# Decode attention with an MLP beside it on one core: the last 4 KB of each row of w1 in three loads of 112, 8 and 8 rows

## The chip, the core and the metric

The kernel runs on one core of one Trainium2 chip. The metric is the time of one execution in device microseconds; for the kernel before it is the median of three runs. The core has five engines that run beside each other: TensorE (PE; PEld is its weight load), VectorE (DVE), ScalarE (ACT), GpSimd (POOL) and SyncE (SP), which here does nothing but issue loads. Sixteen DMA engines move the data between HBM and the on-chip buffers, which have 128 rows (partitions).

## The reference

One token `x` of 512 values is normalised, and two branches are added to it: attention over a cache of 65536 positions, with 32 query heads on 8 heads of keys and values, and an MLP with 1792 hidden values and a ReLU.

```python
x  = A_x                                   # 1 x 512
xn = layernorm(x)
q  = (xn @ wq) as 32 heads of 128          # wq: 512 x 4096
o  = softmax(q k^T * 128**-0.5) v          # k, v: 8 x 65536 x 128; 4 query heads share one of them
y  = x + o @ wo + relu(xn @ w1) @ w2       # wo: 4096 x 512, w1: 512 x 1792, w2: 1792 x 512
```

All is float32. The cache has 2 x 268 MB, the four weights 24 MB together, and there is one token: nearly every byte is read once and used once.

## The kernel before

The program is one function; the engines' programs stand in it one after another, and semaphores by name tie them together. SP issues all the large loads into three buffers, in the order in which the data is used (lines 151 to 179): the three pieces of wq into `kt`, all of w1 into `wt` with one load (line 160), then k and v by turns, 32 pieces of each, k into `kt` and v into `vt`, then wo into `kt`, and w2 in five pieces into `wt`. Each piece of k or v has 128 rows of 64 KB, 8.39 MB. A load counts its semaphore up by 16 when it has landed.

What sets the order around the change is SP's own order: its loads go into one queue, and each DMA engine takes its share of them in that order. SP waits only where a buffer is to be free: `kfree` (line 161, for the first piece of k, when PE is through with wq; then in each turn, when the scores of a piece of k are worked out), `vfree` (line 164), and `hT` (line 174) before w2 overwrites `wt`. At the end it waits for `y` and stores the result.

The row of w1 that lies in a partition has four parts of 1792 values, one for each of the four values of `xn` in that partition. POOL waits for the semaphore `w1` (line 217), multiplies each part by its value of `xn` (line 219) and adds the four to one row of 1792 values (lines 222 to 224), which ends with semaphore `sum`. PE sums that row over the partitions with matmuls by ones (line 281), three times over in each turn, as `PASSES` says, while DVE and ACT do the softmax; the first of them waits for `sum`.

In each turn PE does the matmuls of the scores (line 313), DVE transposes them (366) and takes the maximum (384), ACT takes the exponentials (256), and PE multiplies them with v (292). At the end PE adds the rows of w2 (lines 331 and 339, which wait for each of its five pieces), DVE transposes the sum (417), and SP stores it.

Of the kernel before, what the change touches and what calls it, by code (L numbers as in the profile page):

```python
# [15 lines left out]
DFF_ALL = 1792  # L16
# [21 lines left out]
XA = D // P  # L38
# [6 lines left out]
W2_SUM = 12  # L45
W2_ROWS = 10
PASSES = 3


def take(e, sem, n=1):  # L50

    return e.sem_inc(sem, -n).wait_op(sem, n, "sem-ge")  # L52
# [7 lines left out]
def attention_and_mlp_kernel(  # L60
# [12 lines left out]
    sp, pe, dve, act, pool = nc.sync, nc.tensor, nc.vector, nc.scalar, nc.gpsimd  # L73
    scale = float(DH) ** -0.5

    def sbuf(name, *shape):
        return nc.alloc_sbuf_tensor(name, list(shape), F32).ap()
# [3 lines left out]
    def sem(name):  # L81
        if name not in sems:
            sems[name] = nc.alloc_semaphore(name)
        return sems[name]
# [7 lines left out]
    wt = sbuf("wt", P, FB * D)  # L92
# [47 lines left out]
    w1_row = w1.rearrange("p a f -> p (a f)")  # L140
# [16 lines left out]
    for i in range(1, len(WQ_CUTS)):  # L157
        cut = slice(wq_at[i], wq_at[i + 1])
        sp.dma_start(kt[:, cut], wq_row[:, cut]).then_inc(sem(WQ_SEMS[i]), 16)  # L159
    sp.dma_start(wt, w1_row).then_inc(sem("w1"), 16)  # L160
    take(sp, sem("kfree"))
    sp.dma_start(kt, k[0, 0]).then_inc(sem("k"), 16)
    with sp.Fori(0, NCH - 1) as n:
# [50 lines left out]
    after(pool.tensor_copy(qpad[:, :XA], xn), "pool", chain[0]).then_inc(sem("q"), 1)  # L214
    f = DFF_ALL
    w1_of = [wt[:, a * f : (a + 1) * f] for a in range(XA)]
    pool.wait_ge(sem("w1"), 16)
    for a in range(XA):
        last = pool.tensor_scalar_mul(w1_of[a], w1_of[a], xn[:, a : a + 1])  # L219
    last.then_inc(sem("pool"), 1)  # L220
# [50 lines left out]
    with nc.body("turns", valid_engines=[pe.engine]):  # L271
# [3 lines left out]
        with pe.If(t > 1):  # L275
            after(pe.transpose(pma[:GROUP, :P], m, ident), "d2p").then_inc(sem("p2d"), 1)  # L276
            after(pe.matmul(pmb[:, :GROUP], ones[:GROUP, :], dg, start=True, stop=True), "d2p", 2).then_inc(sem("p2d"), 1)  # L277

            with pe.Fori(0, PASSES):
                for c in range(CT):  # L280
# [175 lines left out]
```

## Time and profile before

| what | value |
|---|---|
| time, median of three runs | 1303.06 us (1302.93 to 1303.19) |
| the profiled execution, first to last instruction (span) | 1301.3 us |
| read from HBM | 560.99 MB, 431 GB/s over the span |
| busy, share of the span: PE | 60% |
| busy: DVE, ACT, POOL | 21%, 6%, 3% |
| DMA engines, in the queue that SP feeds | 99.7% |

The profile has no time of its own for the profiled execution beside its span; the span leaves out what lies ahead of the first instruction and behind the last, and is 1.8 us under the median of the runs. Times in the views are microseconds from the start of the span. A load is shown where it is issued, with the time until it landed; a wait on a load is shown at the instruction that waited.

### The profile page before, as it was taken

To read this page: it belongs to the slowest core of one execution; us is meant where nothing else is said; L and a number is where in the kernel's file an instruction comes from. 1 tells how busy PE (TensorE), PEld (TensorE's weight loads), DVE (VectorE), ACT (ScalarE), POOL (GpSimd) and SP (SyncE) were. 2 spreads that over 40 slices of the span, in tenths; PEclk is the share of its full clock that TensorE was granted. 3 is DMA by queue.
4 is the path that set the end of the run, shared out by engine and by line. 5 is a ranking of instruction groups with operands and counts; after the bars stand their busy time and mean duration, and the time that the engine had idled before them with its cause. 6 is when DMAs were issued, how large, how long until landed. Compare 5 with 4: busy or idle time off the path is not lost.

```text
span 1301.3 us, 13055 instructions
## 1 busy us (share of the span) xinstructions
PE 774.9 (60%) x5474; PEld 231.1 (18%) x5474; DVE 274.8 (21%) x466; ACT 76.2 (6%) x299; POOL 34.8 (3%) x30
## 2 busy tenths in 40 slices
PE   3365674665576456566555566666567466557557
PEld 1111121111121111121111121111112111112112
DVE  2211222211222220222220122221122221122222
ACT  1000000000000000000000000000000000000000
POOL 1900000000000000000000000000000000000000
PEclk9677877776887777786776777677777777777779
DMA  9999999999999999999999999999999999999998
GB/s 403 451 419 451 419 451 419 435 435 419 451 419 451 419 451 419 449 421 423 447 419 451 419 451 419 451 419 435 435 419 451 419 451 419 451 419 443 427 420 370
DMA packets 11236, 561.02 MB, mean 431 GB/s; under 512 B 1505, under 2 KB 1505, under 8 KB 1890
## 3 DMA queue, kind: packets, MB, share of 16 engines
q1 hardware_dynamic: 11088, 561.00, 99.7%
q10 hardware_dynamic: 146, 0.00, 0.0%
q8 instruction: 1, 0.02, 0.0%
q14 instruction: 1, 0.01, 0.0%
HBM read 560.99 MB, written 0.00 MB: 431 GB/s over the span
## 4 chain that ended last, share of the span: by engine, by line
issue 94%; DMA 3%; POOL 2%; SPq 0%; PE 0%; DVE 0%; POOLq 0%
DMA wt<-w 3%; POOL wt L219 1%; POOL wt L224 0%; POOL wt L222 0%; POOL wt L223 0%; SPq L177 0%; SPq L159 0%; PE banks L339 0%; DVE ysb L417 0%; SPq L151 0%; POOL hT L226 0%; SPq L452 0%; POOLq L156 0%
## 5 line engine op out<-in xcount | busy, mean ns | idle before, releaser
L313 PE MATMUL banks<-kt,qpad 128*32 128x512 f32 x2176 | 310.0, 733 | 311.1 <-PEq L52 308.7
L292 PE MATMUL banks<-vt,probs 128*16 128x512 f32 x2048 | 271.3, 690 | 82.1 <-PEq L52 82.1
L366 DVE STREAM_TRANSPOSE tr<-banks 128x1024 f32<-128x1024 f32 x136 | 170.0, 1250 | 471.4 <-PE banks L313 466.8
L313 PEld LDWEIGHTS banks<-kt,qpad 128*32 128x32 f32 x2176 | 84.5, 131 | 509.6 <-issue 496.3
L281 PE MATMUL banks<-wt,ones 128*1 128x448 f32 x768 | 121.3, 786 | 0.0
L292 PEld LDWEIGHTS banks<-vt,probs 128*16 128x16 f32 x2048 | 68.4, 108 | 298.4 <-issue 298.4
L392 DVE COPY o_sb<-banks 128x512 f32<-128x512 f32 x32 | 22.1, 692 | 455.3 <-PE banks L292 455.3
L254 ACT ACTIVATE corr<-diff 128x8 f32<-128x8 f32 x32 | 6.7, 208 | 1179.8 <-ACTq L52 1179.8
L256 ACT ACTIVATE probs<-tr,nb_new 128x128 f32<-128x128 f32 x128 | 65.3, 521 | 0.0
L276 PE MATMUL banks<-ident,m 128*4 128x128 f32 x32 | 9.7, 303 | 78.9 <-DVE m L384 78.9
L302 PE MATMUL banks<-sel,o_sb 128*128 128x4 f32 x256 | 32.8, 252 | 18.7 <-PEq L52 18.7
L302 PEld LDWEIGHTS banks<-sel,o_sb 128*128 128x128 f32 x256 | 31.0, 191 | 20.6 <-issue 20.6
L226 POOL TENSOR_SCALAR hT<-ysum 128x14 f32<-128x14 f32 x1 | 0.3, 257 | 1220.7 <-DVE ysum L404 1220.7
L384 DVE TENSOR_REDUCE m<-tr 128x4 f32<-128x512 f32 x32 | 32.2, 1006 | 2.9
L281 PEld LDWEIGHTS banks<-wt,ones 128*1 128x1 f32 x768 | 20.2, 100 | 58.9 <-issue 58.4
L277 PE MATMUL banks<-dg,ones 4*128 4x4 f32 x64 | 15.4, 309 | 20.0 <-DVE dg L387 20.0
L256 ACT ACTIVATION_READ_ACCUMULATOR probs<-tr,nb_new 128x1 f32 x128 | 24.0, 187 | 0.0
L276 PEld LDWEIGHTS banks<-ident,m 128*4 128x4 f32 x32 | 2.6, 81 | 108.0 <-DVE m L384 108.0
L219 POOL TENSOR_SCALAR wt<-wt,xn 128x1792 f32<-128x1792 f32 x4 | 19.1, 4797 | 16.5 <-DMA wt<-w 16.5
L277 PEld LDWEIGHTS banks<-dg,ones 4*128 4x128 f32 x64 | 12.6, 245 | 27.1 <-DVE dg L387 27.1
L299 PEld LDWEIGHTS banks<-part_sum,ones 128*128 128x128 f32 x64 | 9.5, 188 | 27.2 <-issue 27.2
L395 DVE TENSOR_TENSOR lo_run<-lo_run,banks 128x8 f32<-128x8 f32 x32 | 5.2, 163 | 40.0 <-DVEq L52 40.0
(69 smaller groups left out, 91.1 us busy)
## 6 DMA issues: line engine op xcount, KB each, us to landing
kt<-wq SPq DMA_DIRECT2D x2, 2048.0 KB, 9.3
kt<-wq SPq DMA_DIRECT2D x1, 4096.0 KB, 20.8
kt<-wo SPq DMA_DIRECT2D x1, 4096.0 KB, 15.5
kt<-wo SPq DMA_DIRECT2D x2, 2048.0 KB, 22.2
wt<-w SPq DMA_DIRECT2D x1, 3584.0 KB, 28.9
wt<-w SPq DMA_DIRECT2D x1, 1536.0 KB, 9.5
wt<-w SPq DMA_DIRECT2D x1, 1024.0 KB, 11.7
kt<-k SPq DMA_DIRECT2D x32, 24.1
```

The lines of the kernel that those rows point to most:

```text
L219: last = pool.tensor_scalar_mul(w1_of[a], w1_of[a], xn[:, a : a + 1])
L256: last = act.activation(probs[:, :, g], tr[:, :, g], AF.Exp, bias=nb_new[:, g : g + 1], scale=scale, accum_out=part_sum[:, g : g + 1],)
L276: after(pe.transpose(pma[:GROUP, :P], m, ident), "d2p").then_inc(sem("p2d"), 1)
L277: after(pe.matmul(pmb[:, :GROUP], ones[:GROUP, :], dg, start=True, stop=True), "d2p", 2).then_inc(sem("p2d"), 1)
L281: ins = pe.matmul(hrow[32 * c : 32 * c + 1, :], ones[:, :1], hb[:, :, 32 * c : 32 * c + 32], start=True, stop=True,)
L292: last = pe.matmul(acc[c : c + WIDE * GROUP, :], probs[:, b : b + WIDE, :].rearrange("p b g -> p (b g)"), vt[:, b * DH : (b + WIDE) * DH], ...
L299: pe.matmul(lo_new[:, 0, :], ones, part_sum, start=True, stop=True).then_inc(sem("vfree"), 1)
L302: last = pe.matmul(lo_new[:, 1, :], o_sb[:, b, :], sel[:, b, :], start=(b == 0), stop=(b == WIDE - 1),)
L313: last = pe.matmul(pair[s // 2 % 2][32 * c : 32 * c + 32, s % 2 * 512 : s % 2 * 512 + 512], qpad, kb[:, s * 16 : s * 16 + 16, c, :], start ...
L366: ins = after(dve.transpose(tr2[:, s * 1024 : (s + 1) * 1024], pair[s % 2]), "p2d", s + 1)
L384: dve.reduce_max(m, tr.rearrange("p b i -> p i b")[:, :GROUP, :], axis=AX.X).then_inc(sem("d2p"), 1)
L392: after(dve.tensor_copy(o_sb.rearrange("p b d -> p (b d)"), acc), "p2d", 7).then_inc(sem("d2p"), 1)
```

## The change

The load of w1 is cut in two at 24 KB of each row's 28 KB. The first 24 KB of all 128 rows come as one load. The last 4 KB of each row (1024 values) come as three loads: of rows 0 to 111, of rows 112 to 119, and of rows 120 to 127. All four count the same semaphore, and POOL waits for 64 in place of 16. Bytes, destinations and all else stay as they were. By the words of the change, eight DMA engines are to have nine rows of the 4 KB pieces and eight seven, where a load of 128 rows gives each engine eight.

```diff
+W1_REST = 1024
+W1_ROWS = [slice(0, 112), slice(112, 120), slice(120, 128)]
...
-    sp.dma_start(wt, w1_row).then_inc(sem("w1"), 16)
+    wide = XA * DFF_ALL - W1_REST
+    sp.dma_start(wt[:, :wide], w1_row[:, :wide]).then_inc(sem("w1"), 16)
+    for rows in W1_ROWS:
+        sp.dma_start(wt[rows, wide:], w1_row[rows, wide:]).then_inc(sem("w1"), 16)
     take(sp, sem("kfree"))
     sp.dma_start(kt, k[0, 0]).then_inc(sem("k"), 16)
...
-    pool.wait_ge(sem("w1"), 16)
+    pool.wait_ge(sem("w1"), 16 + 16 * len(W1_ROWS))
```

On SP, between the last load of wq and the first load of v, the kernel before has these instructions (the shape is that of the part of the buffer that is written; the ISA row is a change of a semaphore):

```order
L159 DMA kt<-wq 128x4096
L159 DMA kt<-wq 128x8192
L160 DMA wt<-w 128x7168
L162 DMA kt<-k 128x16384
L163 UNCONDITIONAL_BRANCH
L165 ISA
L165 DMA vt<-v 128x16384
```

And in the same place the changed kernel, whose lines stand two to five further down:

```order
L161 DMA kt<-wq 128x4096
L161 DMA kt<-wq 128x8192
L163 DMA wt<-w 128x6144
L165 DMA wt<-w 112x1024
L165 DMA wt<-w 8x1024 x2
L167 DMA kt<-k 128x16384
L168 UNCONDITIONAL_BRANCH
L170 ISA
L170 DMA vt<-v 128x16384
```

One instruction has become four; the load of k behind them waits for `kfree` in both. No instruction of another engine has moved.

## Rows read from the trace of the kernel before

**Rows 1.** The page: span, DMA share in forty slices (tenths), SP's queue.

```profile
span 1301.3 us, 13055 instructions
...
DMA  9999999999999999999999999999999999999998
...
q1 hardware_dynamic: 11088, 561.00, 99.7%
```

**Rows 2.** The windows view of the middle, columns named in its first line.

```profile
core 0: us, PE busy (x) PEld busy (x) DVE busy (x) ACT busy (x) POOL busy (x), PEclk, DMA share, GB/s
100.00:1260.00 1160.00, 705.28 (x4950) 210.03 (x4950) 240.60 (x418) 67.13 (x270) 0.00 (x0) 0.75 1.00 434
```

**Rows 3.** The timeline of SP: start, duration, what is issued.

```profile
2.22 0.69 SPq L160 DMA_DIRECT2D wt<-w  x1
26.46 0.33 SPq L162 DMA_DIRECT2D kt<-k  x1
27.18 0.34 SPq L165 DMA_DIRECT2D vt<-v  x1
65.47 0.34 SPq L167 DMA_DIRECT2D kt<-k  x1
77.53 0.33 SPq L165 DMA_DIRECT2D vt<-v  x1
```

**Rows 4.** The lines that load v (first) and k (second), issue to landing.

```profile
L165 SPq DMA_DIRECT2D vt<-v x31: 332/333/343, 27.2 to 1201.6; - x31
...
DMA to landing us min/median/max: 28.4/29.3/42.6
...
L167 SPq DMA_DIRECT2D kt<-k x31: 332/333/343, 65.5 to 1225.9; - x31
...
DMA to landing us min/median/max: 23.5/24.1/25.3
```

**Rows 5.** The chain that ended last, its end: start, duration, what.

```profile
1285.18 12.80 DMA wt<-w
...
1298.02 0.44 PE banks L339 x8
...
1298.49 0.41 DVE ysb L417
```

**Rows 6.** The windows view of the end of the stream, columns as in rows 2.

```profile
1297.00:1297.10 0.10, 0.10 (x14) 0.04 (x4) 0.10 (x1) 0.00 (x0) 0.00 (x0) 1.00 0.96 348
...
1297.20:1297.30 0.10, 0.10 (x8) 0.00 (x0) 0.08 (x1) 0.00 (x0) 0.00 (x0) 1.00 0.26 82
1297.30:1297.40 0.10, 0.10 (x8) 0.07 (x8) 0.00 (x0) 0.00 (x0) 0.00 (x0) 1.00 0.22 82
1297.40:1297.50 0.10, 0.10 (x8) 0.09 (x12) 0.00 (x0) 0.00 (x0) 0.00 (x0) 1.00 0.06 21
```

**Rows 7.** The timeline at the end: PE's weight loads that waited for w2.

```profile
1292.94 0.11 PEld L331 LDWEIGHTS banks<-wt,hT 128*1 128x1 f32 x8 [2.54 <-DMA wt<-w]
...
1295.44 0.16 PEld L331 LDWEIGHTS banks<-wt,hT 128*1 128x1 f32 x8 [0.70 <-DMA wt<-w]
...
1296.72 0.32 PEld L339 LDWEIGHTS banks<-wt,hT 128*1 128x1 f32 x16 [1.12 <-DMA wt<-w]
...
1298.02 0.10 PEld L339 LDWEIGHTS banks<-wt,hT 128*1 128x1 f32 x8 [0.36 <-DMA wt<-w]
```

**Rows 8.** The timeline of ACT's queue: the load of x into one row.

```profile
1.40 0.53 ACTq L235 DMA_DIRECT2D xrow<-x  x1
```

**Rows 9.** The timeline of POOL on w1, and of PE behind it.

```profile
31.17 19.12 POOL L219 TENSOR_SCALAR wt<-wt,xn 128x1792 f32<-128x1792 f32 x4 [16.46 <-DMA wt<-w]
...
58.39 3.99 POOL L224 TENSOR_TENSOR wt<-wt 128x1792 f32<-128x1792 f32 x1
...
64.23 4.66 PE L281 MATMUL banks<-wt,ones 128*1 128x448 f32 x24
69.91 7.06 PE L292 MATMUL banks<-vt,probs 128*16 128x512 f32 x64 [1.02 <-PEq L52]
```

## The prediction

> **What bounds the kernel now.** I read the page first for what is busy: the sixteen DMA engines are at 9 tenths or more in all but the last of the forty slices, and the one queue that SP feeds fills 99.7% of their time [rows 1]. The windows view of the long middle says the same with a rate: DMA share 1.00 at 434 GB/s over 1160 us, which is 27.1 GB/s for one engine, while PE is busy for 705 of the 1160 us [rows 2]. So the time is that of a stream of 561 MB, and it can be lost in two ways only: an engine has nothing queued, or an engine has more to move than the others.
>
> The first does not happen. The issues on SP and the times to landing show it [rows 3, 4]: the first load of v is issued at 27.18 us and lands 42.6 us later (the longest of its kind), at 69.8; the next load of k is issued at 65.47. So 4.3 us before the queue would be empty the next 8 MB is behind it. A load of v is issued 28.4 to 42.6 us before it lands and a load of k 23.5 to 25.3 us, where one of them takes 8.39 MB / 434 GB/s = 19.3 us; the shortest of these covers is 23.5 - 19.3 = 4.2 us.
>
> The second is what the change is about. What ends the program is the last piece of w2: the chain shows it landing 12.80 us after its issue at 1285.18, so at 1297.98, then PE from 1298.02, DVE from 1298.49 and the store [rows 5]. Everything behind that landing is fixed. Since each engine works through its queue without a pause, whatever an engine is given more near the start arrives as a later landing at the end, unless another engine is later anyway. The end of the stream shows how even they are [rows 6]: at 1297.0 to 1297.1 rows of 2 KB still start at 348 GB/s, at 1297.2 to 1297.3 at 82 GB/s (8.2 KB, four rows), at 1297.3 to 1297.4 again four, at 1297.4 to 1297.5 one. An engine starts a row about every 81 ns (below), so after 1297.2 three or four engines are left, and the last of them is 0.2 to 0.3 us behind the bulk. That is all that a perfect evening-out of the engines could give: under 0.3 us of 1303, 0.02%.
>
> **The change, part by part.** Prices first, from loads of 128 rows, so eight rows an engine. PE's weight loads at L331 and L339 wait for the pieces of w2 one after another [rows 7]: the second piece (8 KB rows) is there 2.50 us after the first (1295.44 - 1292.94), so 312 ns a row; the third (4 KB rows) 1.28 us later, so 160 ns a row; the last two (2 KB rows, sixteen rows an engine) 1.30 us later, 81 ns a row. From 4 KB to 8 KB it is 152 ns for 4 KB more, so a row costs 8 ns beside its bytes (160 - 152), or, if this belongs to the load and not to the row, a load costs 8 x 8 = 64 ns.
>
> Moved bytes: an engine had eight rows of 28 KB. Now it has eight of 24 KB, and of the 4 KB rows seven (from the load of 112) or nine (seven, and one from each load of eight rows). Eight engines gain a row, +152 ns; eight lose one, -152 ns.
>
> Added pieces: the seven-row engines have fifteen rows where they had eight and two loads for one: 7 x 8 = 56 ns, or 64 ns. The nine-row engines have seventeen rows and four loads: 9 x 8 = 72 ns, or 3 x 64 = 192 ns. So the seven-row engines come to -0.09 us, and the nine-row engines to +0.22 to +0.34; I take +0.25, nearer to the price by rows, since the rows of 2 KB, with a load for each eight, leave only 81 - 76 = 5 ns.
>
> What this does to the end hangs on which engines are the three or four late ones; no row says. If they are among those with seven rows, they end 0.09 us earlier and the bulk of the others, 0.2 to 0.3 us ahead of them, moves up by 0.25: end between -0.09 and +0.14. If one of them has nine rows, the end is +0.22 to +0.34. I take +0.15 us over both. Below nothing it cannot go by more than the 0.15 us of one row.
>
> Issue on SP: three more instructions. The load of w1 took 0.69 us to issue, the one-row load of x on ACT 0.53 [rows 3, 8]; 3 x 0.69 = 2.1 us at most. SP is then done at about 5.0 us in place of 2.9; its next instruction is held by a semaphore until 26.46, and the engines come to w1 only after wq, whose queue is full until then. Cost nothing; it would cost if wq had landed before 5 us.
>
> The wait on POOL: it waits for all four loads (64 in place of 16), behind it stand four multiplications and three additions, 31.17 to 62.38, and who waits for them is PE at L281, which starts at 64.23 because DVE is that late [rows 9]. So 1.85 us of delay are hidden there, and a further 0.9 us or so between the end of L281 (68.89) and the first matmul on v (69.91). A landing 0.3 us later costs nothing; above 2.7 us the first issue of v would move, which has its own cover (it is issued at 77.53, while the load of k ahead of it lands no sooner than 65.47 + 23.5 = 89.0).
>
> The span is 1301.3 us and the median of the runs is 1303.06, 1.8 us more for what lies around it; the sum goes onto the median: 1303.06 + 0.15 = 1303.2.
>
> **The rivals.** (1) The small loads run slower than their rows in a full load. All loads that this trace prices have 128 rows, and there 27.1 GB/s may be the limit of the engine or of the place where its rows land; the rows cannot tell these apart, because each engine always serves the same sixteenth of the rows. If it is the place, eight neighbouring rows crowd together. Bounds: spread over eight places, 160 ns a load (the forecast); in one place, eight rows in turn, 1.28 us a load, 2 x (1.28 - 0.16) = +2.24 us for both. With two places it is 4 x 160 = 640 ns a load and 2 x 0.48 = +0.96. The engines with nine rows then end 0.96 + 0.25 later than they did, and they are the last; less what they were ahead, +1.0 to +1.2, so 1304.2. For it speaks that engine rate and place rate could not be told apart in any row; against it, that a row shows no such slowing. [...]
>
> (2) Slower by what can be measured: the crowding is complete. Each load of eight rows goes in turn (+2.24), the load of 112 rows, which no longer falls on the engines as 128 rows do, meets itself in pairs (7 x 160 ns = +1.12), and +0.25 as above: +3.6 us, 1306.7. It decides from 2.6 us on. Against it: the sixteen engines never showed such a loss in any slice.
>
> (3) The change does not do what it says: a load of eight rows is given to one engine, not to eight. That engine has 23 rows of 4 KB in place of eight: 15 x 160 = +2.4 us and the pieces, 1305.5. [...]
>
> (4) A gain that can be measured, 2.6 us. The stream has no idle time to give back and the late engines are under 0.3 us behind; I see no mechanism.
>
> **How the numbers follow.** About 0.2% (2.6 us) is what a measurement of this kernel can tell from no change. Forecast 0.55 (1302.95 to 1303.4); rival (1) 0.36 (up to 1304.7 with some of the load of 112 rows slowed too); (3) 0.03; (2) 0.03; another slowing, such as a queue that runs dry, 0.02; (4) 0.01. Forecast and rival (1) together hold 0.91 and lie within 0.2%; with the 0.02 of them that reach further I take 1302.85 to 1304.6 as the range. Rival (3) lies just under the bound and counts as the same, the other slowing half to each side: same 0.91 + 0.03 + 0.01 = 0.95, slower 0.04, faster 0.01.
>
> **What would show it.** In the profile after: the weight loads at L331 and L339 waiting for w2 at the same distances (2.50, 1.28, 1.30 us), all shifted by one amount; the multiplications on POOL starting at about 31.4 if the forecast holds, at 32.2 to 32.5 with two places; the tail of the stream after 1297.2 with about eight engines in it, not four. The forecast is wrong if POOL's start moves by over 0.5 us, and its argument is wrong if POOL's start moves and the end does not, for then the stream has slack that I don't see.

## The result, and the profile after

| | before | changed |
|---|---|---|
| time, median of 21 runs | 1303.31 us | 1305.31 us (1304.87 to 1305.84) |
| ratio, 95% interval | | 1.0016 (1.001 to 1.0021) |
| span of the profiled execution | 1301.3 us | 1303.2 us |

The kernel became 2.0 us slower: under the 0.2% (2.6 us) that I had named as the least difference to be told, but clear of its own interval, and outside the range of the prediction, which ended at 1304.6.

The page of the changed kernel, beside [rows 1]: the engines' queue is as full as it was, the bytes are the same, but there are 11396 DMA packets, where the page before had 11236.

```profile
span 1303.2 us, 13058 instructions
...
DMA packets 11396, 561.02 MB, mean 431 GB/s; under 512 B 1537, under 2 KB 1537, under 8 KB 2050
...
q1 hardware_dynamic: 11248, 561.00, 99.7%
```

Now the start, in the timelines of SP, POOL and PE of the changed kernel (start, duration, what; beside [rows 3, 9]):

```profile
2.22 0.65 SPq L163 DMA_DIRECT2D wt<-w  x1
2.91 1.23 SPq L165 DMA_DIRECT2D wt<-w  x3
26.57 0.36 SPq L167 DMA_DIRECT2D kt<-k  x1
...
32.52 19.12 POOL L224 TENSOR_SCALAR wt<-wt,xn 128x1792 f32<-128x1792 f32 x4 [17.73 <-DMA wt<-w]
...
59.75 3.98 POOL L229 TENSOR_TENSOR wt<-wt 128x1792 f32<-128x1792 f32 x1
...
64.74 2.44 PE L286 MATMUL banks<-wt,ones 128*1 128x448 f32 x24
70.99 9.45 PE L297 MATMUL banks<-vt,probs 128*16 128x512 f32 x60 [3.81 <-PEq L54]
```

w1 is there 1.35 us later than before (POOL at 32.52, not 31.17), and the first piece of v is late too: the first matmul on v starts at 70.99, not 69.91. So the stream lost about 1.1 us around these three loads, and the 1.1 us stay. The windows view shows how (columns as in rows 2):

```profile
29.50:30.40 0.90, 0.00 (x0) 0.00 (x0) 0.00 (x0) 0.00 (x0) 0.00 (x0) 0.50 1.07 323
...
31.00:31.50 0.50, 0.00 (x0) 0.00 (x0) 0.00 (x0) 0.00 (x0) 0.00 (x0) 0.50 1.49 533
```

From 29.5 to 30.4, with rows of 4 KB alone, the share of 1.07 goes with 323 GB/s: 16 x 4096 B x 1.07 / 323 = 217 ns of an engine for a row, where such a row of w2 took 160 [rows 7]. From 31.0 to 31.5 the engines start four rows of 64 KB (the first of k) and one of 4 KB (533 GB/s x 0.5 us) and are held 1.49 x 16 x 0.5 = 11.9 us by them, so 2.9 us by a row of 64 KB; in the middle it is 16 x 65.5 KB / 434 = 2.42 [rows 2]. Busy engines, then, that move less; what their rows wait for is not in these windows.

The end of the chain (beside [rows 5]) and the store, of the changed kernel; the store's row has the size and the us from issue to landing:

```profile
1285.73 13.27 DMA wt<-w
1299.01 0.04 issue
1299.05 0.44 PE banks L344 x8
1299.52 0.41 DVE ysb L422
```

```profile
y<-ysb SPq DMA_DIRECT2D x1, 2.0 KB, 2.4
```

The last piece of w2 lands at 1299.00, 1.0 us later than before; that is the stream's loss. But the store takes 2.4 us to land. In the page of the kernel before it took 1.4:

```profile
y<-ysb SPq DMA_DIRECT2D x1, 2.0 KB, 1.4
```

By these two profiles the 2.0 us are two halves: 1.0 to 1.1 in the stream, and 1.0 in the store at the very end, which the change does not touch.

### The profile page after: what moved, and what is told of

It is laid out like the page before. It is cut to its first block, busy times and chain, and to the rows that moved or that the text cites. A ratio compares the mean times of both kernels' runs of the same rounds, so it can differ in the third digit from the quotient of the medians.

```text
span 1303.2 us, 13058 instructions
## 1 busy us (share of the span) xinstructions
PE 775.1 (59%) x5474; PEld 230.3 (18%) x5474; DVE 274.7 (21%) x466; ACT 76.3 (6%) x299; POOL 34.8 (3%) x30
## 2 busy tenths in 40 slices
DMA packets 11396, 561.02 MB, mean 431 GB/s; under 512 B 1537, under 2 KB 1537, under 8 KB 2050
## 4 chain that ended last, share of the span: by engine, by line
issue 94%; DMA 3%; POOL 2%; SPq 0%; PE 0%; DVE 0%; POOLq 0%
DMA wt<-w 3%; POOL wt L224 1%; POOL wt L227 0%; POOL wt L229 0%; POOL wt L228 0%; SPq L182 0%; SPq L165 0%; SPq L161 0%; SPq L163 0%; PE banks L344 0%; DVE ysb L422 0%; SPq L153 0%; POOL hT L231 0%; SPq L457 0%; POOLq L158 0%
## 5 line engine op out<-in xcount | busy, mean ns | idle before, releaser
L297 PE MATMUL banks<-vt,probs 128*16 128x512 f32 x2048 | 278.0, 704 | 88.8 <-PEq L54 88.8
L286 PE MATMUL banks<-wt,ones 128*1 128x448 f32 x768 | 116.8, 760 | 0.0
L389 DVE TENSOR_REDUCE m<-tr 128x4 f32<-128x512 f32 x32 | 32.2, 1006 | 2.9
```

The source lines that it names most:

```text
L286: ins = pe.matmul(hrow[32 * c : 32 * c + 1, :], ones[:, :1], hb[:, :, 32 * c : 32 * c + 32], start=True, stop=True,)
L297: last = pe.matmul(acc[c : c + WIDE * GROUP, :], probs[:, b : b + WIDE, :].rearrange("p b g -> p (b g)"), vt[:, b * DH : (b + WIDE) * DH], ...
L389: dve.reduce_max(m, tr.rearrange("p b i -> p i b")[:, :GROUP, :], axis=AX.X).then_inc(sem("d2p"), 1)
```

## The experiments

Two questions. For the stream: theory *place* (a rate belongs to where rows land, and neighbouring rows crowd) against theory *engine* (each DMA engine has its own rate). For the store: what makes it late. In the tables "first matmul on v" is where PE starts on the first piece of v (69.91 before) and reads the stream's loss without the noise of the end; "store" is its time to landing; "runs" is the median against that of the kernel before on the same chip, in us.

How far these numbers carry: the four profiles of kernels that leave the start as it was (the kernel before twice, its store issued by ACT, one load of w2 less) have the first matmul on v at 69.91, 69.97, 70.08 and 70.15, so 0.25 us is not told from nothing there. The end of one profile is worse: with the store issued by ACT the last piece of w2 was waited for until 1298.88 in place of 1298.02, though the runs were the same. And the medians are of 8 to 12 runs; the 95% interval of such a difference reaches 1.1 to 1.4 us to either side, so differences up to +1.3 are not clear of nothing by the runs alone, and are read together with the profile.

**The changed kernel again.** No edit.

> The changed kernel once more, unaltered, for a second profile. Its first profile has the last piece of w2 landing at 1299.01, 1.03 us later than before, but the span is 1.9 us longer: the store at the end, issued at 1299.95, took 2.4 us to land where before it took 1.4. Theory A (the stream alone is what the change costs, the slow store is chance): last piece of w2 again about 1.0 later than before, store 1.4, span 1302.4, and the runs a little over 1.0 us slower than before on the whole. Theory B (the late store belongs to the change): store 2.4 again, span 1303.2, runs 2.0 us slower.

Measured: first matmul on v at 71.30, last piece of w2 waited for until 1299.36, store 2.5 us, runs +1.8 (1305.32 against 1303.50; 1.0014, 1.0005 to 1.0023). The late store belongs to the change. Its counterpart, the kernel before again:

> The kernel before, unaltered, for a second profile. In its first profile the store took 1.4 us to land; in the four kernels with changed loads it took 2.3 to 2.9. Theory chance (the first profile was a lucky one, and the late store has no cause in the loads): 2.0 us or more here too, span 1302 or more. Theory belonging (the quick store belongs to this program): 1.4 to 1.6 again, span 1301.3 to 1301.7. The last piece of w2 lands at 1297.98 within 0.1 in either.

Measured: 69.97, store 1.4, runs -0.06. The quick store belongs to the program before.

**Four extra loads of 8 rows, neighbouring or spread.** The kernel before with its single load of w1, and behind it:

```diff
+    for i in range(N_EXTRA):                       # 4
+        cut = slice(i * 1024, (i + 1) * 1024)
+        sp.dma_start(junk[112:120, cut], w1_row[112:120, cut]).then_inc(sem("w1"), 16)
...
-    pool.wait_ge(sem("w1"), 16)
+    pool.wait_ge(sem("w1"), 16 + 16 * N_EXTRA)
```

and in the other kernel `0:32:4` in place of `112:120`, twice.

> The kernel before with its one load of w1, and behind it four extra loads of 8 rows x 4 KB, each of rows 112 to 119 of w1 once more into a buffer that nothing reads (128 KB more are moved; the result is untouched). Theory place (a rate belongs to where rows land, and eight neighbouring rows share two places): 4 x 640 = 2.56 us for eight engines, so the last piece of w2 lands 2.3 to 2.6 us later than before. Theory engine (each DMA engine has its own rate, wherever the rows lie): 4 x (160 + up to 64) = 0.64 to 0.9 us, last piece 0.5 to 0.9 later. POOL starts on w1 later by as much.

> The same as the run with four extra loads of 8 rows x 4 KB, but of every fourth row from 0 to 28 instead of 112 to 119; bytes, loads and rows an engine are the same. Theory place: these eight rows lie in eight places, so 4 x 160 to 224 ns, last piece of w2 0.5 to 0.9 us later than before, 1.8 us or so less than with the neighbouring rows. Theory engine: the same 0.5 to 0.9, no difference between the two runs.

The timeline of PE, neighbouring rows, then spread rows:

```profile
73.10 7.06 PE L297 MATMUL banks<-vt,probs 128*16 128x512 f32 x64 [0.75 <-PEq L53]
```

```profile
70.51 7.06 PE L297 MATMUL banks<-vt,probs 128*16 128x512 f32 x64 [0.84 <-PEq L53]
```

The same bytes, loads and rows an engine cost 3.2 us in rows 112 to 119 (2.3 to 2.6 expected by theory place) and 0.6 us in every fourth row: 0.65 us more for each load, where two places would make it 0.48. Runs +3.5 and +1.4. Theory engine falls. It also settles rival (3): eight rows to one engine would be 4 x 8 x 160 ns = 5.1 us in both.

The windows in which the engines start their first rows of k show on whom the crowding falls. In this order: the kernel before, the changed kernel, neighbouring rows, spread rows (columns as in rows 2):

```profile
30.30:30.80 0.50, 0.00 (x0) 0.00 (x0) 0.00 (x0) 0.00 (x0) 0.00 (x0) 0.50 4.89 2097
```

```profile
30.40:31.30 0.90, 0.00 (x0) 0.00 (x0) 0.00 (x0) 0.00 (x0) 0.00 (x0) 0.50 3.71 1274
```

```profile
30.40:30.61 0.21, 0.00 (x0) 0.00 (x0) 0.00 (x0) 0.00 (x0) 0.00 (x0) 0.50 11.84 2633
```

```profile
30.30:31.30 1.00, 0.00 (x0) 0.00 (x0) 0.00 (x0) 0.00 (x0) 0.00 (x0) 0.50 2.75 1176
```

Before, sixteen rows of 64 KB (2097 GB/s x 0.5 us) hold the engines 39.1 us, 2.44 us a row. In the changed kernel it is sixteen such rows and 24 of 4 KB (1274 x 0.9) and 53.4 us; less 24 x 0.217 that leaves 3.0 us a row. In the record of the single packets each of these sixteen rows took 2.84 to 3.20 us, where before each took 2.42 to 2.48. So all sixteen engines lose 0.4 to 0.8 us in their first row of k, nearly 0.6 on the mean, not only the eight with nine rows of w1. With neighbouring rows, eight rows of 64 KB and seven of 4 KB start in the third window (2633 x 0.21) and hold 39.8 us, about 4.8 us for a row of 64 KB. The profile names no engine; by the order of the queue these are the eight without a row of the extra loads, and the other eight, still at those, start on k from 31.2 to 33.1. With spread rows (sixteen rows of 64 KB and 31 of 4 KB in the fourth window, 44.0 us) it is 2.44 us a row again. So the crowded loads held up engines that had no part in them; that is more than theory place says, in which eight rows wait for each other.

**64 rows twice; 112 and 16 rows; four full loads.** The last 4 KB in two loads of rows 0 to 63 and 64 to 127, in two of rows 0 to 111 and 112 to 127, or w1 in four loads of all 128 rows:

```diff
+    for rows, cols in W1_PARTS:
+        sp.dma_start(wt[rows, cols], w1_row[rows, cols]).then_inc(sem("w1"), 16)
```

> The last 4 KB of each row of w1 in two loads of 64 rows each (0 to 63, 64 to 127), the first 24 KB in one load of 128: three loads, and each engine has eight rows of 4 KB in all, as before. Theory engine: two loads and eight rows more, 8 x 8 to 2 x 64 = 64 to 128 ns, last piece of w2 0.06 to 0.13 us later than before. Theory place (64 neighbouring rows reach half of the places): each of the two loads takes 8 x 160 = 1.28 us where it would take 0.64, so 1.28 us more, last piece 1.3 to 1.4 later, all engines alike.

> The last 4 KB of each row of w1 as two loads, of rows 0 to 111 and of rows 112 to 127, so each engine has eight rows again; the first 24 KB in one load. Theory place: 16 neighbouring rows share four places, so that load takes 4 x 160 = 0.64 us in place of 0.16, and the 112 rows meet in pairs part of the time (0.1 to 0.4 us): last piece of w2 0.6 to 1.0 us later than before. Theory engine: 0.06 to 0.13 later. Store: 1.4 if its delay belongs to engines that are out of step (here they are in step), 2.4 if it belongs to any added load.

> w1 in four loads as in the change, but all of 128 rows: 6144, 512, 256 and 256 values of each row. Same bytes and eight rows an engine in each load; only the pieces are added: 24 rows more an engine, 24 x 8 ns or 3 x 64 ns = 0.19 us. Both theories of place and engine: last piece of w2 0.15 to 0.25 us later than before. Store: 2.4 us if three more loads in the queue are enough to make it late, 1.4 if it takes neighbouring rows or engines out of step.

| loads of w1 | first matmul on v | later by | store | runs |
|---|---|---|---|---|
| 64 and 64 rows | 71.41 | 1.5 | 2.9 | +2.6 |
| 112 and 16 rows | 71.08 | 1.2 | 2.8 | +2.5 |
| the change: 112, 8, 8 | 70.99, 71.30 | 1.1, 1.4 | 2.4, 2.5 | +2.0, +1.8 |
| four of 128 rows | 70.23 | 0.3 | 3.3 | +1.75 |

In the first two every engine has eight rows of 4 KB, as before, and still 1.2 to 1.5 us are lost (1.3 to 1.4 and 0.6 to 1.0 expected by theory place): it is the rows that are taken together, not the uneven engines. Four full loads, as many as in the change, lose 0.1 to 0.3 and no more, which does not contradict the price of pieces (0.15 to 0.25 expected). But their store is the latest of all, 3.3 us, though every load has all 128 rows: the late store has another cause.

**Loads of 16 bytes.** Extra loads of 1, 8 or 16 rows of 16 bytes into a buffer that nothing reads, behind the load of w1:

```diff
+    for i in range(N_EXTRA):
+        sp.dma_start(junk[:16, i * 4 : i * 4 + 4], w1_row[:16, i * 4 : i * 4 + 4]).then_inc(sem("w1"), 16)
```

> The kernel before and, behind its load of w1, three extra loads of one row x 16 bytes into a buffer that nothing reads. The stream is as long as before (three rows of 16 bytes on one engine, under 0.06 us), only the number of loads and instructions on SP is that of the change. If the late store comes with the mere number of loads or with the program's size: store 2.4 us, span 1302.3, runs 0.8 to 1.0 slower than before. If it comes with what the loads do to the engines: store 1.4, runs within 0.1 us of before.

> The kernel before and, behind its load of w1, four extra loads of 16 rows x 16 bytes into a buffer that nothing reads: one row an engine, so each of the 16 engines has 8 DMA packets more ahead of the store (a row and a closing packet for each load), and under 0.1 us more to do. Theory count (an engine's store lands late or not by how many packets it had before: +8, +10, +12 and +27 were late, 0 and +6 not): the store takes 2.2 to 2.9 us, span about 1302.3, runs 0.7 to 1.1 slower than before. Theory bytes (it takes loads that lengthen the stream): 1.4, runs within 0.15 of before.

> The same with eight such loads, so 16 packets more an engine and under 0.2 us more to do. Theory count with a period of 16 packets (684 packets stand before the store in the kernel before; the late cases all have the store's nine packets across places 11 to 12 of 16, the others not): the store takes 1.4 us again, span 1301.4 to 1301.6, runs 0.1 to 0.2 slower than before, faster than with four loads. Theory that every added load on all engines makes it late: 2.4, runs 0.9 or more slower.

> The same with four loads of 8 rows x 16 bytes, so only eight engines have 8 packets more. Theory count: of the store's sixteen landings eight come in time and eight late, the store takes 2.2 us or so, runs 0.6 to 1.0 slower than before. Theory bytes: 1.4 and all in time.

> The changed kernel and, behind its loads of w1, four extra loads of 16 rows x 16 bytes. The change itself gives eight engines 12 and eight engines 8 packets more than before; with these it is 20 and 16. Theory count with a period of 16: both are places where the store is in time, so the store takes 1.4 us, the stream stays about 1.1 us longer than before, span 1302.4 to 1302.6, runs 1.0 to 1.3 slower than before, and so 0.7 to 1.0 FASTER than the changed kernel, though it does more. Theory stream (the late store is owed to the crowded loads): 2.4 again, runs 2.0 to 2.2 slower than before.

> The kernel before with three extra loads of 16 rows x 16 bytes behind its load of w1: 6 packets more on each of the 16 engines, one step under the run with four (8 more, store 3.1 us). Theory limit (the store of an engine is late once more than a certain number of packets went through SP's queue on that engine before it, between 6 and 8 more than in the kernel before): store 1.4 us, runs within 0.2 of before. Theory any load on all engines: store 2.3 or more, runs 0.8 to 1.3 slower.

Four loads of 16 rows (8 packets more an engine) leave the stream alone and make the store twice as slow; rows of its timeline of PE and its DMA view:

```profile
70.02 8.76 PE L296 MATMUL banks<-vt,probs 128*16 128x512 f32 x64 [2.32 <-PEq L53]
```

```profile
y<-ysb SPq DMA_DIRECT2D x1, 2.0 KB, 3.1
```

Runs +1.2 (1304.62 against 1303.39). Three loads of one row: store 1.4, runs +0.2 within their scatter (1302.91 to 1303.93). My theory of a period of 16 packets fell: with 16 more the store took 2.9 us (runs +2.1, and the stream lost 1.0, which I had not expected of eight such loads and cannot explain), and the changed kernel with four more loads was slower, not faster (store 2.8, runs +2.6). What was left is a limit that, once passed, stays passed. Eight-row loads, so that half of the engines pass it: 2.3 us, runs +0.75. Six packets more on each engine: 2.7 us, runs +0.8, so my limit between six and eight fell too. Yet the three loads of one row, six packets more in all (on a single engine, if one took them all), left the store quick.

The traces keep the landing of each of the store's sixteen increments of its semaphore, and not the last alone. The store's own packets are not late: the last goes out about 1.03 us after the issue in the kernel before, in the changed kernel and with four loads of 16 rows. In the six profiles with a quick store all sixteen increments are there within 0.42 us of that packet. With four loads of 8 rows (neighbouring, spread, 16 bytes) 8, 8 and 7 of them are, and the rest come up to 1.36 us behind it; with three loads of 16 rows 10 are, with four such loads none, in the changed kernel 3. So it goes by engine (where half of the engines have more packets, about half of the increments are late), and it is the completion that is late, not the data. But the limit is not sharp: with 27 packets more on each engine (four full loads) 4 increments still come in time.

**One load less, or another queue.** The changed kernel with the last two pieces of w2 in one, and its control; the changed kernel with the store issued by ACT, and its control; and the loads of 16 bytes issued by ACT.

```diff
-W2_CUTS = [6, 4, 2, 1, 1]
+W2_CUTS = [6, 4, 2, 2]
```

```diff
-    sp.wait_ge(sem("y"), 1)
-    sp.dma_start(out.rearrange("(p a) -> p a", p=P), ysb[:, 0, :]).then_inc(sem("ends"), 16)
...
+    act.wait_ge(sem("y"), 1)
+    act.dma_start(out.rearrange("(p a) -> p a", p=P), ysb[:, 0, :]).then_inc(sem("ends"), 16)
```

> The changed kernel with the last two pieces of w2 loaded as one (pieces of 6, 4, 2, 2 blocks in place of 6, 4, 2, 1, 1): one load less, 9 packets less an engine, so 3 more on eight engines and 1 less on eight than in the kernel before. PE then has two blocks to multiply after the last landing, not one, 0.3 to 0.5 us more there. Theory limit: store 1.4 us, and the runs 0.4 to 0.7 faster than the changed kernel in spite of PE's longer end. Theory that neighbouring rows or engines out of step make the store late: store 2.4 again, runs 0.3 to 0.5 slower than the changed kernel.

> The kernel before with the last two pieces of w2 loaded as one: the control of the changed kernel with that edit. 9 packets less an engine. All theories: store 1.4 us; PE's end after the last landing longer by 0.2 to 0.4, the landing 0.06 earlier or the same: runs 0.1 to 0.4 slower than before. The changed kernel with this edit was 1.0 slower than before, so the stream's part of the change would be 0.6 to 0.9.

> The changed kernel with the store at the end issued by ACT, whose queue has carried two loads before it, and not by SP. Theory limit in SP's queue: store 1.4 us or little more, span 1302.2 to 1302.6, runs 1.0 to 1.3 slower than before and 0.7 to 1.0 faster than the changed kernel. Theory of memory or of the engines themselves (the store is late in whatever queue): 2.4 or more, runs 1.9 to 2.1 slower than before.

> The kernel before with the same edit, the store issued by ACT: what the edit does by itself. All theories: store 1.3 to 1.5 us, runs within 0.2 us of before. If it is slower here by x, x is to be taken off the run of the changed kernel with this edit.

> The kernel before with four extra loads of 16 rows x 16 bytes into a buffer that nothing reads, issued by ACT at its start, so that 8 packets more go through each DMA engine but none through SP's queue. Theory engine count (what counts is an engine's packets, in whatever queue): store 2.3 to 3.1 us, runs 0.7 to 1.2 slower than before. Theory SP count (only packets in SP's queue count): store 1.4, runs within 0.2 of before.

With one load less the changed kernel keeps its crowded loads (first matmul on v at 71.10) and has its quick store back; its page and DMA view:

```profile
DMA packets 11252, 561.02 MB, mean 431 GB/s; under 512 B 1521, under 2 KB 1521, under 8 KB 1906
```

```profile
y<-ysb SPq DMA_DIRECT2D x1, 2.0 KB, 1.4
```

It is 1.0 us slower than the kernel before (1304.42 against 1303.41), so 0.8 to 1.0 faster than the changed kernel (0.4 to 0.7 expected); the same edit in the kernel before costs 0.06 (1303.33 against 1303.27; 0.1 to 0.4 expected). So the stream's part is about 1.0 us and the store's the other 0.8 to 1.0. From ACT's queue the store of the changed kernel is as late (2.6 us, runs +2.3), in the kernel before it is 1.5 there (runs -0.04); loads of 16 bytes issued by ACT make it late as well (3.0 us, runs +1.3). So neither the store's queue nor SP's alone is what counts. Of all the profiles, sorted by the packets that the page counts:

| DMA packets on the page | kernel | store, us |
|---|---|---|
| 11092 | before, one load less | 1.4 |
| 11236 | before, twice; store by ACT | 1.4, 1.4, 1.5 |
| 11242 | three loads of one row | 1.4 |
| 11252 | changed, one load less | 1.4 |
| 11300, 11300, 11301 | 4 loads of 8 rows: neighbouring, spread, 16 bytes | 2.3, 2.4, 2.3 |
| 11332 | three loads of 16 rows | 2.7 |
| 11364, 11364 | four loads of 16 rows by SP, by ACT | 3.1, 3.0 |
| 11396 | changed, twice; store by ACT; 64 and 64; 112 and 16 | 2.4, 2.5, 2.6, 2.9, 2.8 |
| 11492, 11524 | eight loads of 16 rows; changed with four | 2.9, 2.8 |
| 11668 | four full loads of w1 | 3.3 |

No kernel at or under 11252 packets has a late store, none at or over 11300 a quick one. It is not the chip: on each of the chips 6, 7 and 9 there are kernels of both kinds. But another count sorts these kernels as well: the packets under 512 B, 1489 to 1521 with a quick store and 1537 to 1761 with a late one. No run tells whether all packets count or the small ones. And the runs add up to 0.6 us less than stream and store together (four loads of 16 rows: 0.1 + 1.7 against +1.2): a profile is one execution. No version was faster than the kernel before.

## Why the prediction was wrong

**What bounds the kernel** was right: the stream does not pause, and what it lost at 30 us was still missing at the end (POOL 1.35 later, PE's first matmul on v 1.1, the last piece of w2 1.0). The distances of the pieces of w2 stayed, as the prediction had named for a sign: PE's weight loads wait until 1293.97, 1296.45, 1297.76 and 1299.05, so 2.48, 1.31 and 1.29 us.

**The cost of issue and the wait on POOL** were right: SP took 0.65 + 1.23 us and was done at 4.1, its next load went out at 26.57; POOL was through with w1 at 59.75 + 3.98 = 63.73, and PE came to it at 64.74.

**The price of the small loads** was the first failed step: +0.15 us for the end of the stream, where the run with one load less shows 1.0. I had both ends, 0 and +2.24 us for the two loads of eight rows, and took the lower one because the nearest row was that of a 4 KB row in a full load. That row holds nothing about neighbouring rows: all the loads that I had priced have 128 rows, as rival (1) itself said. And forecast and rival alike went engine by engine, as if what a row costs fell on the engine that moves it. The windows at 30 us show otherwise: all sixteen engines lose time in their first row of k, nearly 0.6 us on the mean.

Rival (1) with two places gave +1.0 to +1.2 for the end of the stream (its terms, 0.96 + 0.25 less up to 0.3, make 0.9 to 1.2); measured 1.0 and, in the second profile, 1.3. POOL started at 32.52 and 32.80, where its sign was 32.2 to 32.5. That its number is so near is in part luck. By its account the eight engines with nine rows are more than 1 us behind the other eight, so that the last microsecond of the stream has half of the engines and some 217 GB/s. In the changed kernel, whose last rows start just under 1298.50:

```profile
1297.30:1297.70 0.40, 0.27 (x4) 0.00 (x0) 0.07 (x1) 0.00 (x0) 0.00 (x0) 1.00 1.07 399
```

```profile
1298.20:1298.30 0.10, 0.10 (x8) 0.00 (x0) 0.10 (x1) 0.00 (x0) 0.00 (x0) 1.00 0.29 102
```

A microsecond before its end the stream still moves 399 GB/s, and in its last 0.3 us five rows start in 0.1 us where it was four [rows 6], so not the eight engines that the prediction had named as a sign either. The engines stayed about as even as they were; all of them are late.

Rival (1)'s case of two places was an assumption: no run shows in how many places eight rows land, nor the four places for 16 rows and the half of them for 64 that the expectations take. That each engine always serves the same sixteenth of the rows was assumed as well; the profile names no engine. What the runs showed in its place: a load of rows 112 to 119 cost 0.65 us more than one of spread rows, where two places at 160 ns a row would make it 0.48, so the direction was right and the size nearly. That the engines without a row in such a load lose nearly as much (4.8 us for a row of 64 KB in place of 2.44, behind four of them) is not in that sum. And one reservation: in each pair the rows that were read in HBM moved with the rows that were written, and no run held the one and moved the other. So by these pairs it is neighbouring rows that cost the stream its 1.0 us; whether by where they land or by where they come from, and what the other engines wait for, is open.

**"Everything behind that landing is fixed"** was the second failed step, and the one that took the time out of the range. With the stream's part alone the time is 1304.4, as the run with one load less shows, inside the range. The store at the end, which I had put at no change, took 2.4 and 2.5 us in place of 1.4 and costs nearly the same again. This goes with the number of packets and not with how the loads of w1 crowd. Nothing in the trace before hinted at it, since there the store takes 1.4 us; but the change raised a count, and I priced the pieces by their time alone. Rival (2), a loss of over 2.6 us in the stream, was not reached: measured 1.0 to 1.4, not 3.6.

**The evening-out** that could have given 0.1 us is not to be seen under this.

What stays open is what counts the packets. On the page the change-over lies between 11252 and 11300. By engine it lies above the three more that eight engines of the changed kernel with one load less have, in time, and under the eight more that make about half of the increments late where half of the engines have them; six more on each engine made 6 of 16 late. It concerns the store, which writes HBM, and not the loads of w2 just ahead of it: with four loads of 16 rows the last piece is waited for until 1298.11, against 1298.02 before. Each packet is also an entry of the profile, and no run tells whether the recording has a part in it.

## What to carry to other kernels

In a stream that never pauses, cut loads along the bytes of a row and keep all 128 rows in each: four full loads of w1 cost 0.1 to 0.3 us of stream, one full load with two or three that have some of the rows 1.1 to 1.5. Even so the four were 1.75 us slower than one, by the late store: a cut that gives nothing back is best left out. Here every engine paid for the crowded loads (2.84 to 3.20 us for its first row of k in place of 2.42 to 2.48), which a sum engine by engine misses. When the price of an operation lies between two ends and the nearest row does not contain the thing in question, take the middle or name the forecast undecided; a row can be near in size and far in kind. And look at what a change counts up, not only at what it takes: here what went with 160 more packets was worth nearly as much as the crowding, and one load less elsewhere bought that half back.

## What the runs showed of the hardware that was not expected

The store of 2 KB took 1.4 to 1.5 us or 2.3 to 3.3, and which of the two went, in these kernels, with the number of packets on the page, 11252 at most or 11300 at least, whether SP or ACT issued them (the table above). Behind four loads of eight neighbouring rows, engines without a row in them took 4.8 us for a row of 64 KB in place of 2.44.

In five of the profiles (neighbouring rows, spread rows, 64 and 64 rows, four full loads, eight loads of 16 bytes) the end was set by PE, not by the last load. The granted clock from 1283 to 1300 us was 0.80 with neighbouring rows and with 64 and 64 rows, 0.84 with four full loads and 0.83 with spread rows (0.50 up to about 1288.8, and 1.00 from there),

```profile
1283.00:1300.00 17.00, 14.71 (x126) 4.18 (x126) 7.91 (x10) 0.00 (x0) 0.26 (x1) 0.83 0.86 359
```

where the kernel before and the changed kernel have 1.00 in the same stretch. Ahead of it PE did the same in the kernel before and with spread rows (64 matmuls on v, ten small ones, 1.77 us idle); why the clock fell in the one is not in the rows. Of the changed kernel:

```profile
1283.00:1300.00 17.00, 12.50 (x126) 3.58 (x126) 7.72 (x10) 0.00 (x0) 0.26 (x1) 1.00 0.89 371
```

So of the +2.6 and +3.5 of 64 and 64 rows and of neighbouring rows a few tenths may be PE's (in their profiles DVE's last transpose is 2.0 and 3.6 us later than before, the first matmul on v 1.5 and 3.2), and the stream is better read at the first matmul on v. And eight loads of 16 rows x 16 bytes cost the stream 1.0 us (first matmul on v at 70.87), four of them nothing (70.02).
